# Linear attention and SwiGLU on one core: the weights loaded at other times, and 1/den of two groups spread by PE

## The chip, the core and the metric

The kernel runs on one core of a Trainium2 chip. The metric is the device time of one execution in microseconds. Five engines work beside each other, each with its own queue of instructions that it takes in order: TensorE (PE, the matrix engine), VectorE (DVE), ScalarE (ACT), GpSimd (POOL) and SyncE (SP, which here only issues DMAs). They wait for each other through semaphores.

## The reference

A sequence x of 2048 tokens of 512 numbers in bf16 passes four layers. Layers 0 and 2 are linear attention A, layers 1 and 3 the feed-forward part B, with the same weights both times:

```
phi = lambda t: where(t > 0, t + 1, exp(t)) + 1e-6
A(x): q, k, v = split(x @ wqkv)                 # 32 heads of 16
      kv  = sum_s phi(k)_s v_s^T ;  z = sum_s phi(k)_s          # per head
      o   = (phi(q) @ kv) / (phi(q) @ z + 1e-6)
      return o @ wo
B(x): return (silu(x @ w_gate) * (x @ w_up)) @ w_down            # 512 -> 1792 -> 512
x = x + A(layernorm(x)); x = x + B(layernorm(x)); the same two again
```

The layer norm has neither scale nor offset, with eps 1e-5.

## The kernel before

The sequence is cut into 16 tiles of 128 tokens, four of them to a group of 512. All weights and x stay in SBUF. x is loaded by SyncE, K's part of the weights by ScalarE, Q's part by SyncE behind x, and everything else (V's part `Wv`, `Wo`, `Wg`, `Wu`, `Wd`) by GpSimd in layer 0.

The work is written as operations with reads and writes (`op`, a class `Prog`). The order of PE is written out by hand in the string `PROGRAM`; every other engine's order comes from the kernel's own list scheduler (`schedule`), which takes, among the operations that can start within `HOLD` of the earliest, the one with the smallest due time, shifted by `BIAS` for its kind. `sync` then places the semaphore waits. DMAs of SyncE take turns on eight lanes, and each waits for the one eight before it; GpSimd's take turns on four. `ON_ACT` lists the operations that ScalarE does instead of VectorE.

A token of `PROGRAM` is a layer, a letter and indices. `S` is a matmul of zeros at the start, which nobody reads. The letters:

- `t` (0t0): a tile is transposed by PE (`xt_pe`); tiles that are not in `PE_T` are transposed by a DMA of SyncE from the normalised tile `xnA` or `xnB` into `xnT` (L506).
- `k`: K of a tile, four matmuls, then phi (`phi`: ScalarE exp L539, VectorE L544, then L551, or ScalarE L542 and VectorE L548) into `pk`.
- `g`, `z`: what a tile adds to pk^T x and to the sum of pk. In place of V, the normalised x is summed up, and `v` (`kvt`) multiplies by Wv afterwards, masks the result to single heads on VectorE (L612, `KVT`), and `m` multiplies it by Wo. Both results are copied out of PSUM into `GT` (L599 ScalarE, L602 VectorE).
- `q` (0q03: group 0, quarter 3): Q of a group, and phi into `pq`.
- `d` (0d03): phi(q) times z, that is den. After the fourth quarter of a group VectorE adds 1e-6 (L651) and takes the reciprocal (L654, `rtok`). For each tile ScalarE then writes 1/den 16 times beside itself (L661, `rrep`), a DMA of SyncE transposes this into `RT` (L665), and VectorE multiplies pq by it (L674).
- `w` (0w0): the output of an attention tile, pq times GT; VectorE adds it to x and sums the row up (L696). The next layer's norm follows: ScalarE sums the squares (L473), GpSimd makes mean, variance and rstd (L476, L482, L486), VectorE (L497) or ScalarE (L493) applies them, and the transpose goes to SyncE's queue.
- `u` (1u011: group 0, block 11 of 128 hidden columns), `n`: the FFN, eight matmuls and a tanh each (L716, L718, L721), and the down projection of a tile (L744).

Nearly all matmuls are recorded in the helper `mm`, so they stand under L388; PE's transposes stand under L520. Layer 0's norm takes its sums from VectorE (L462, L464).

The weights that GpSimd loads are held back until one transpose of layer 0 has landed:

```python
last = [o for o in pr.ops if o.kind == "xT"][-1:]
for w_ in weights:
    w_(last)
```

The list is in the order of tiles, so that one is tile 15's, which is not the last that SyncE issues.

## Time and profile before

| what | us |
|---|---|
| median of 6 runs | 435.76 |
| lowest and highest | 433.6, 437.88 |
| the profiled execution: its time | 435.6 |
| its span, from the first to the last instruction | 433.7 |
| PE busy | 420.3 |
| VectorE busy | 294.4 |
| ScalarE busy | 203.0 |
| GpSimd busy | 79.9 |

The span is what the profile covers; 1.9 us of the execution lie around it. An engine's busy time is the union of its instructions. A wait is put down to the semaphore that came last. The chain of waits is followed back from the last instruction, at each step to what released it.

### The profile page before, as it was taken

To read this page: it belongs to the slowest core of one execution; us is meant where nothing else is said; L and a number is where in the kernel's file an instruction comes from. 1 tells how busy PE (TensorE), PEld (TensorE's weight loads), DVE (VectorE), ACT (ScalarE), POOL (GpSimd) and SP (SyncE) were. 2 spreads that over 40 slices of the span, in tenths; PEclk is the share of its full clock that TensorE was granted. 3 is DMA by queue.
4 is the path that set the end of the run, shared out by engine and by line. 5 is a ranking of instruction groups with operands and counts; after the bars stand their busy time and mean duration, and the time that the engine had idled before them with its cause. 6 is when DMAs were issued, how large, how long until landed. Compare 5 with 4: busy or idle time off the path is not lost.

```text
span 433.7 us, 6518 instructions
## 1 busy us (share of the span) xinstructions
PE 420.3 (97%) x2195; PEld 193.5 (45%) x2195; DVE 294.4 (68%) x594; ACT 203.0 (47%) x381; POOL 79.9 (18%) x230
## 2 busy tenths in 40 slices
PE   7997998999999999999999999899999999999997
PEld 3443443444444444444444454344444444444444
DVE  6975789895498457884754548898855617744762
ACT  4875786944454254442525758486322203411320
POOL 5754117303310120002002100642020000000000
DMA  8479644320210010000101105443010010001001
GB/s 279 84 142 369 208 89 82 77 59 14 48 36 2 12 36 2 0 2 12 26 12 24 26 15 104 78 87 73 1 38 24 12 39 12 14 13 36 2 0 50
DMA packets 57249, 24.29 MB, mean 56 GB/s; under 512 B 50752, under 2 KB 56000, under 8 KB 57216
## 3 DMA queue, kind: packets, MB, share of 16 engines
q1 hardware_dynamic: 55232, 16.79, 18.1%
q0 software_dynamic: 1440, 6.55, 4.4%
q10 hardware_dynamic: 544, 0.52, 0.4%
q8 instruction: 18, 0.29, 0.3%
q14 instruction: 15, 0.12, 0.1%
HBM read 9.70 MB, written 2.10 MB: 27 GB/s over the span
## 4 chain that ended last, share of the span: by engine, by line
PE 82%; DMA 5%; DVE 5%; POOL 3%; ACT 2%; issue 2%; SPq 2%; DVEq 0%; ACTq 0%
PE pb L388 82%; DMA xnT<-xnA 2%; POOL rstd L486 1%; SPq L506 1%; DVE X L696 1%; DMA xnT<-xnB 1%; DMA RT<-rrep 1%; DVE pq L674 1%; DMA X<-in_A_x_dram 1%; DVE GT L602 1%; DVE xnB L497 1%; ACT etmp L539 0%; POOL vpe L482 0%; DVE rtok L654 0%; ACT xnA L493 0%
## 5 line engine op out<-in xcount | busy, mean ns | idle before, releaser
L716 ACT ACTIVATE tht<-pb 128x512 f32<-128x512 f32 x112 | 66.6, 594 | 120.1 <-PE pb L388 113.9
L388 PE MATMUL pb<-xnT,Wg 128*128 128x512 bf16 x448 | 115.0, 379 | 1.3 <-DMA xnT<-xnB 1.3
L388 PE MATMUL pb<-xnT,Wu 128*128 128x512 bf16 x448 | 115.0, 379 | 0.0
L388 PE MATMUL pb<-Wd,hT 128*128 128x512 bf16 (+1 forms) x462 | 99.3, 373 | 0.0
L718 DVE SCALAR_TENSOR_TENSOR tht<-tht,pb 128x512 f32<-128x512 f32 x112 | 76.8, 686 | 28.6 <-ACT tht L716 25.9
L721 DVE TENSOR_TENSOR hT<-tht,pb 128x512 bf16<-128x512 f32 x112 | 77.0, 688 | 11.6
L388 PEld LDWEIGHTS pb<-Wd,hT 128*128 128x128 bf16 x462 | 45.2, 98 | 51.5
L388 PEld LDWEIGHTS pb<-xnT,Wg 128*128 128x128 bf16 x448 | 43.7, 98 | 54.3 <-issue 1.8
L388 PEld LDWEIGHTS pb<-xnT,Wu 128*128 128x128 bf16 x448 | 43.8, 98 | 52.9
L476 POOL TENSOR_SCALAR mv<-sums 128x1 f32<-128x1 f32 x48 | 11.4, 242 | 228.7 <-DVE X L696 130.7
L539 ACT ACTIVATE etmp<-pb 128x512 bf16<-128x512 f32 x64 | 38.1, 598 | 30.1 <-PE pb L388 29.7
L486 POOL TENSOR_TENSOR rstd<-vpe,negh 128x1 f32<-128x1 f32 x64 | 36.8, 575 | 5.3
L388 PE MATMUL pb<-Wqkv,xnT 128*128 128x512 bf16 x128 | 31.8, 379 | 3.5 <-DMA xnT<-xnA 3.5
L388 PE MATMUL pb<-GT,pq 128*128 128x512 bf16 x128 | 31.2, 380 | 2.8 <-DVE pq L674 2.4
L744 DVE SCALAR_TENSOR_TENSOR pq<-pb,X 128x512 bf16<-128x512 f32 (+1 forms) x17 | 11.2, 660 | 32.7 <-PE pb L388 32.7
L388 PE MATMUL pb<-xnT,Wqkv 128*128 128x512 bf16 x128 | 32.2, 378 | 0.0
L388 PE MATMUL pb<-pk,xnA 128*128 128x512 bf16 x128 | 31.7, 378 | 0.4 <-DVE pk L551 0.4
L473 ACT ACTIVATE xnB<-X,sums 128x512 bf16<-128x512 bf16 x32 | 22.9, 716 | 14.7 <-DVE X L696 7.5
L544 DVE TENSOR_SCALAR etmp<-etmp 128x512 bf16<-128x512 bf16 x64 | 18.9, 296 | 14.5 <-ACT etmp L539 13.7
L744 DVE SCALAR_TENSOR_TENSOR X<-pb,X 128x512 bf16<-128x512 f32 x16 | 11.1, 692 | 20.5 <-PE pb L388 20.5
L473 ACT ACTIVATE xnA<-X,sums 128x512 bf16<-128x512 bf16 x16 | 11.5, 720 | 23.8 <-DVE X L744 23.7
L661 ACT ACTIVATE rrep<-rtok 128x512 bf16<-128x512 bf16 x32 | 18.7, 622 | 6.7 <-DVE rtok L654 5.1
(63 smaller groups left out, 302.3 us busy)
## 6 DMA issues: line engine op xcount, KB each, us to landing
out_dram<-pq SPq DMA_DIRECT2D x15, 128.0 KB, 1.7
Wg<-in_B_w_gate_dram POOLq DMA_DIRECT2D x4, 448.0 KB, 5.7
Wu<-in_B_w_up_dram POOLq DMA_DIRECT2D x4, 448.0 KB, 5.4
X<-in_A_x_dram SPq DMA_DIRECT2D x6, 256.0 KB, 4.9
Wd<-in_B_w_down_dram POOLq DMA_DIRECT2D x3, 512.0 KB, 5.5
Wqkv<-in_A_wqkv_dram ACTq DMA_DIRECT2D x2, 256.0 KB, 3.5
X<-in_A_x_dram SPq DMA_DIRECT2D x4, 128.0 KB, 3.4
Wqkv<-in_A_wqkv_dram SPq DMA_DIRECT2D x1, 512.0 KB, 6.4
```

The costliest lines, as they stand in the source:

```text
L388: return op("pe", lambda e: e.matmul(o_ap, lhsT=lhsT, rhs=rhs, start=start, stop=stop, skip_group_check=skip), r=r, w=w, occ=occ, lat=occ ...
L473: op("act", lambda a: a.activation(out=b_ap, in_=X[:, t, :], func=ACT.Square, scale=-float(D), bias=sums[:, t:t + 1], accum_out=mv[:, t, 1 ...
L476: op("pool", lambda p: p.tensor_scalar(out=mv[:, t, 0:1], in0=sums[:, t:t + 1], scalar1=-1.0 / D, scalar2=None, op0=ALU.mult), r=[f"sm{t}" ...
L486: op("pool", lambda p: p.tensor_tensor(out=rstd[:, t:t + 1], in0=vpe[:, t:t + 1], in1=negh[:], op=ALU.pow), r=[f"vp{t}", "negh"], w=[f"rs{ ...
L497: op("dve", lambda v: v.tensor_scalar(out=b_ap, in0=X[:, t, :], scalar1=mean, scalar2=rstd[:, t:t + 1], op0=sub, op1=ALU.mult), r=[xk, f"m ...
L539: op("act", lambda a: a.activation(out=etmp[e][:], in_=PB[pb][:], func=ACT.Exp), r=[f"pb{pb}"], w=[f"e{e}"], occ=0.48, lat=0.55, kind="exp")
L544: op("dve", lambda v: v.tensor_scalar(out=etmp[e][:], in0=etmp[e][:], scalar1=1.0, scalar2=1e-6, op0=ALU.min, op1=ALU.add), r=[f"e{e}"], w ...
L661: op("act", lambda a, tl=tl, q=q: a.activation(out=rrep[q][:].rearrange("p (h j) -> p h j", j=DH), in_=rtok[d][:, tl * H:(tl + 1) * H].uns ...
L716: op("act", lambda e: e.activation(out=tht[a][:], in_=PB[pg][:], func=ACT.Tanh, scale=0.5), r=[f"pb{pg}"], w=[f"th{a}"], occ=0.48, lat=0.5 ...
L718: op("dve", lambda v: v.scalar_tensor_tensor(out=tht[a][:], in0=tht[a][:], scalar=1.0, in1=PB[pg][:], op0=ALU.add, op1=ALU.mult), r=[f"pb{ ...
L721: op("dve", lambda v: v.tensor_tensor(out=hT[h][:, j, :], in0=tht[a][:], in1=PB[pu][:], op=ALU.mult), r=[f"pb{pu}", f"th{a}"], w=[f"h{h}_{ ...
L744: op("dve", lambda v, pb=pb, lo=lo, hi=hi: v.scalar_tensor_tensor(out=o_ap[:, lo:hi], in0=PB[pb][:, 0:hi - lo], scalar=0.5, in1=X[:, t, lo ...
```

## The change

- The load of `Wv` goes from GpSimd to SyncE, behind that of Q's weights and ahead of the transposes.
- `Wo`, `Wg` and `Wu` wait for all DMA transposes of layer 0, and stand in the order Wo, four Wg, four Wu in GpSimd's queue.
- `Wd` is loaded by GpSimd after the first four output tiles of layer 0 (`load_down`); its first load waits for the transposes of layer 1's first group.
- Group 2 of layer 0 and group 1 of layer 2 no longer go over `rrep` and the DMA. VectorE transposes `rtok` in blocks of 32 x 32 into `rT`, and PE multiplies `rT` by a constant `esel` (ScalarE writes its four parts once) in four steps `r` of four matmuls each, which spreads 1/den over the 16 columns of a head. VectorE multiplies pq straight from PSUM, in each step the tokens of one block of 32 in every tile. `rep_pe` did this in another form before, and was called by no token.
- Tile 15 of layer 0 is transposed by PE (`0t15`).
- `rrep` has three buffers instead of four.
- PE's order, `ON_ACT`, `BIAS`, `HOLD` and some of the scheduler's estimates are new; with them ScalarE makes the sums of tiles 4 and 8 in layer 0, and VectorE some of the variances. Paths for `raw` tiles and `colsum` are written too; no token uses them.

The diff, cut to its core:

```diff
@@ scheduler's constants, PROGRAM, PE_T, ON_ACT
-HOLD = 0.16
+HOLD = 0.17
...
-S S S S S S S S S 0t0 S S S 0t1 0k0 0t2 0t3 0k1 S 0k2 0z0 0g0 0k3 0g1 0k4 0g2 0g3 0k5 0k9 0z4 0g4 0k10 0g5 0k7
-0z9 0k8 0z2 0q03 0k6 0z7 0g10 0q01 0z8 0k12 0z1 0k15 0k13 0z10 0g9 0z6 0k11 0z3 0q11 0g7 0k14 0z15 0z11 0z5
-0q02 0z13 0q12 0z12 0q21 0z14 0g11 0q00 0q13 0d02 0d03 0q10 0g8 0d00 0g6 0d01 0q20 0d13 0g13 0q22 0d10 0d12
-0d11 0d20 0g12 0q23 0g14 0g15 0q30 0d22 0d21 0d23 0v 0q31 0m0 0m2 0m1 0m3 0q32 0w0 0w2 0q33 0w3 0d32 0w1 0w9
-0w6 0d30 0w10 0w5 0w4 0w7 0d33 0w11 0w8 0d31 1u011 1u009 1u002 1u000 1u012 1u004 1u007 1u005 1u003 1u006 1u013
...
+S S S S S S S S S 0t0 S S S S 0t3 0t1 0k0 0t2 0k1 0k2 0g0 0k3 0z0 0g1 0k4 0g2 0g3 0k5 0z4 0k10 0z2 0k9 0g4 0g5
+0k6 0z10 0k7 0z9 0z3 0q03 0k8 0g10 0t15 0g7 0k15 0k13 0z5 0z8 0k12 0g9 0k11 0q11 0g6 0z15 0k14 0q10 0z13 0q02
+0z7 0z1 0q01 0g11 0q00 0z14 0q12 0q21 0z12 0z6 0z11 0q13 0d02 0d03 0d01 0d00 0g8 0d11 0q20 0g13 0d12 0q22 0d13
+0d10 0q23 0d20 0g15 0g12 0g14 0d23 0d22 0d21 0q30 0v 0q31 0m0 0m1 0m3 0m2 0r21 0r23 0w3 0r22 0w2 0w1 0r20 0w0
+0q33 0w5 0w11 0w7 0w6 0w9 0q32 0d33 0w8 0w4 0w10 1u011 1u007 1u005 1u008 0d31 1u002 1u006 0d32 1u012 1u003
+1u013 0d30 1u010 1u004 1u000 1u110 1u001 1u009 0w14 1n3 0w12 1n0 1u106 1n1 1u102 1n2 1u107 1u204 0w13 1u101
...
-2q31 2g13 2d12 2g8 2q30 2g11 2g15 2g10 2d23 2g9 2q32 2v 2q33 2m1 2m0 2m3 2d31 2m2 2d32 2w0 2w1 2w2 2w3 2w10
-2d30 2w7 2w6 2d33 2w4 2w8 2w11 2w9 2w5 3u008 3u007 3u002 3u000 3u010 2w14 3u004 3u011 3u009 3u005 3u013 3u006
-3u012 3u001 3u103 3u003 3u110 3u108 3u104 2w13 3n3 2w12 3u100 3n2 3n0 3u106 3u105 3u107 3u111 3n1 3u102 3u109
...
+2d22 2q30 2d10 2d12 2g13 2g10 2d11 2d23 2q31 2g15 2g4 2g9 2g11 2g8 2q32 2r10 2v 2q33 2m1 2m0 2m2 2m3 2w0 2d31
+2r11 2d30 2w1 2r13 2w2 2w3 2r12 2w6 2w5 2w11 2w4 2w8 2w7 2d32 2w9 2w10 2d33 3u008 3u000 3u009 3u013 3u010
+3u004 3u003 3u005 3u007 3u103 3u110 3u108 3u012 3u002 3u001 3u006 3u104 2w13 3u011 3n3 2w12 3u100 3n2 3n0
...
 PE_T = set("""
-0t0 0t1 0t2 0t3
+0t0 0t1 0t2 0t3 0d2 0t15 2d1
 """.split())
...
-        rrep = [sb("rrep", [P, 512], BF16) for _ in range(4)]
+        rT = [sb("rT", [P, TG * H], BF16) for _ in range(2)]
+        esel = sb("esel", [P, H, DH], BF16) if any(x[1] == "d" for x in PE_T) else None
+        rrep = [sb("rrep", [P, 512], BF16) for _ in range(3)]
...
+            for i in range(0, P if esel is not None else 0, H):
+                op("act", lambda a, i=i: a.activation(
+                    out=esel[i:i + H], in_=ident[i:i + H, i:i + H].unsqueeze(2).to_broadcast([H, H, DH]),
+                    func=ACT.Copy), r=["ident"], w=[f"esel{i // H}"], occ=0.52, after=after)
...
         dma("sp", Wqkv[:, :, 0:D], wq3[:, :, 0:D], 512, w=["Wq"], prio=-80)
-        weights.append(lambda a: dma("pool", Wqkv[:, :, 2 * D:], wq3[:, :, 2 * D:], 512, w=["Wv"], after=a,
-                                     occ=1.0))
+        dma("sp", Wqkv[:, :, 2 * D:], wq3[:, :, 2 * D:], 512, w=["Wv"], prio=-79)
...
-        for c in range(0, NF, 4):
-            c1 = min(NF, c + 4)
-            weights.append(lambda a, c=c, c1=c1: dma(
-                "pool", Wd[:, c:c1, :], B_w_down[c * P:c1 * P, :].rearrange("(c p) f -> p c f", p=P),
-                128 * (c1 - c), w=[f"Wd{j}" for j in range(c, c1)], after=a, occ=0.75))
+
+        def load_down(after):
+            for c in range(0, NF, 4):
+                c1 = min(NF, c + 4)
+                dma("pool", Wd[:, c:c1, :], B_w_down[c * P:c1 * P, :].rearrange("(c p) f -> p c f", p=P),
+                    128 * (c1 - c), w=[f"Wd{j}" for j in range(c, c1)], after=after, occ=0.75)
...
             if f"{L}d{g}" in PE_T:
+                op("dve", lambda v: v.transpose(out=rT[d][:], in_=rtok[d][:]), r=[f"rtok{d}"], w=[f"rT{d}"],
+                   occ=0.2, lat=0.3, kind="den")
                 return
...
-        def rep_pe(L, g, tl):
+               occ=0.335, lat=0.42, kind="pqn")
+
+        def rep_pe(L, g, a):
 
             pb = bank()
             d = db[L, g][1]
             r_den.done(d)
+            ps = slice(a * H, (a + 1) * H)
             for c in range(NC):
-                lo = tl * H + c * HC
-                mm(pb, rtok[d][:, lo:lo + HC].unsqueeze(2).to_broadcast([P, HC, DH]), ident[:], True, True,
-                   r=[f"rtok{d}", "ident"], w=[f"pb{pb}"], occ=MM128, cols=(c * P, (c + 1) * P), skip=True)
-            scale(L, g, tl, PB[pb][:].rearrange("p (c k) -> p c k", c=NC), f"pb{pb}", 0.607)
+                mm(pb, esel[ps, c * HC:(c + 1) * HC, :].rearrange("p h j -> p (h j)"), rT[d][ps, :], True, True,
+                   r=[f"rT{d}", f"esel{a}"], w=[f"pb{pb}"], occ=MM128, cols=(c * P, (c + 1) * P), skip=True)
+            b = pq_of[L, g]
+            ks = [f"pq{b}_{j}_{tl}" for j in range(NC) for tl in range(TG)]
+            ap = pq[b][:].rearrange("p c (t a i) -> p c t a i", t=TG, a=P // H)[:, :, :, a]
+            by = PB[pb][:].rearrange("p (c t i) -> p c t i", c=NC, t=TG)
+            op("dve", lambda v: v.tensor_tensor(out=ap, in0=ap, in1=by, op=ALU.mult),
+               r=ks + [f"pb{pb}"], w=ks, occ=0.607, lat=0.69, kind="pqn")
...
-        last = [o for o in pr.ops if o.kind == "xT"][-1:]
+        last = [o for o in pr.ops if o.kind == "xT"]
...
+                if tok in head:
+                    head.discard(tok)
+                    if not head:
+                        load_down([xT_of[1, t] for t in range(TG) if (1, t) in xT_of])
```

## The prediction

> **What bounds the kernel now.** I read the page from the top: busy shares, slices, then the waits of PE, then the chain around the longest wait, then single rows for prices.
>
> ```profile
> PE 420.3 (97%) x2195; PEld 193.5 (45%) x2195; DVE 294.4 (68%) x594; ACT 203.0 (47%) x381; POOL 79.9 (18%) x230
> PE   7997998999999999999999999899999999999997
> DMA  8479644320210010000101105443010010001001
> ```
>
> PE is busy 97%. In the 20 us windows between 100 and 260 us it is busy all the time, with 93 to 95 large matmuls in each: 0.214 to 0.216 us per 128x512 matmul, at a granted clock of 1.00. There nothing can be gained or lost but matmuls. The slices that are not nines are the head, two stages of layer 0 (20 to 40 us and 55 to 73 us), the same second stage of layer 2 (slice 24, 260 to 283 us), and the tail. The change is worth what it does there.
>
> ```profile
> PE pb L388 <- DMA xnT<-xnA: 3.5, 2, 2.6
> PE pb L388 <- DVE pq L674: 2.4, 6, 0.6
> PE pb L388 <- DMA xnT<-xnB: 1.3, 2, 1.0
> ```
>
> The waits of PE (us in total, times, longest) name three causes: a DMA transpose of layer 0, the scaling by 1/den, and the first transposes of layers 1 and 3. The chain shows where the longest comes from:
>
> ```profile
> 27.52 0.97 POOL Wqkv L415
> ...
> 28.50 0.76 POOL Wo L415
> ...
> 29.60 0.57 POOL rstd L486
> ...
> 30.27 0.42 DVE xnA L497
> ...
> 30.76 6.83 DMA xnT<-xnA
> 37.59 0.14 issue
> 37.73 2.50 PE pb L388 x25
> ```
>
> GpSimd issues the loads of Wv and Wo before it makes the last tile's rstd; that tile's transpose is issued at 30.76, runs beside the weights, and lands after 6.83 us where the median is 2.4. Step 0k14 waits for it.
>
> **A. From the start to 0v (55.07 us before).** I measure in starts of PE's steps. Between 0k4 (14.10) and 0v lie 40.97 us. Four gaps in it, start to start less the matmuls between (0.864 us per four): 0.19 before 0g2, 0.52 before 0g5, 1.12 before 0k6, 2.74 before 0k14; together 4.57. Work is 36.40.
>
> *Removed.* In the new order GpSimd's first load stands behind the last rstd and waits for all eleven transposes. Tile 15 goes by PE, so eleven are left. They need 1.31 us each in SP's queue (issue to issue where they follow closely); the fourth was issued at 16.46, so by their inputs the last comes at about 25 to 27 and lands by 30. 0k14 now stands 20 large steps behind 0k4, after 32 us: its 2.74 us go. 0k6 waited for the transpose issued at 20.81, which landed after 4.89 us; a 16 KB packet of the instruction queue at 22.0 lies in that stretch. Tile 6 is now the fifth transpose, due at about 18.5, and 0k6 stands at about 22: that wait goes too. What is late next is 0k8 (seventh transpose, 22 undisturbed, 24.4 with the same delay), wanted at about 25: just covered.
>
> *Added.* Four PE transposes for 0t15: 0.24 (0t1 to 0k0: 7.73 to 7.97). The head: 0t3 now stands before 0t1 and waits for the rstd of tile 3, which GpSimd makes after tile 1's; 0k0 moves from 7.97 to about 8.8. Four warm-up matmuls stand behind 0t0 instead of three, but the one before 0k2 is gone. ScalarE takes the sums of tiles 4 and 8 (two Copy and two Square passes at about 0.71) before its copy of 0t3; I get 0k4 at 14.8 by following ScalarE's queue, 0.7 late.
>
> Wv goes on SP's queue behind Wq, ahead of the first transpose. Here a rule speaks against the change. Row: Wq landed at 12.10, 1.45 after the last of x; the first transpose was issued at 11.25, with Wq still moving, and landed at 13.81, after 2.56 instead of 2.44. So a load ahead in the queue cost it 0.12. Wv will move until about 13.55. The Trainium skill (DMA: Bandwidth & Descriptors, "Two DMAs through the same engine are not ordered") says that within one queue of an engine descriptors start in order, but pipelined. By that the transpose starts behind Wv and lands at 13.55 + 2.44 = 15.99, and 0k4 at 16.1; by the row it lands between 13.9 and 15.25. I take the row's middle, 14.6, so 0k4 stays at 14.8. The rule's value would add 1.3 us.
>
> ScalarE's work up to 0v grows: two more normalisations (0.72), four passes for sums, four constants `esel` (0.52 by the slot of L661), less three Identity passes (0.575) and one spread: +4.1 us. It was about 36 busy of 47. I allow 0.3 of new waits; ends 0 and 3. VectorE gets 0.5 less. The weight loads, 4.15 MB at the 260 GB/s of before (4.67 MB from 27.5 to 45.4), run from 29 to about 45.5: Wo and Wg are first wanted after 52 and 67, so they cost nothing; the first spread's transpose comes only then.
> A = −4.57 + 0.24 + 0.7 + 0.3 = −3.3; I use −3.2.
>
> **B. 0v to the first FFN step, layer 0.** Before 55.07 to 73.40 = 18.33 us, with PE's work 15.1.
>
> ```profile
> 55.00:74.00 19.00, 16.68 (x108) 7.89 (x105) 17.29 (x49) 13.95 (x30) 7.46 (x23) 1.00 0.48 89
> 265.00:283.00 18.00, 15.79 (x94) 6.64 (x92) 16.06 (x43) 11.25 (x25) 7.42 (x22) 1.00 0.42 81
> ```
>
> The windows (length; then busy us of PE, PEld, VectorE, ScalarE, GpSimd; clock, DMA share, GB/s) show VectorE busy 91% and 89%: it is the near-bound of both stages, and SP's transposes stand in one queue of 1.31 us each.
>
> Group 2 loses four spreads on ScalarE, four transposes on SP (4 x 1.31 = 5.2 us of that queue) and four scalings from SBUF; it gains a VectorE transpose, 16 matmuls 128x128 on PE and four scalings from PSUM.
>
> ```profile
> L661 ACT ACTIVATE rrep<-rtok 128x512 bf16<-128x512 bf16 x32 | 18.7, 622 | 6.7 <-DVE rtok L654 5.1 <-DMA RT<-rrep 1.5
> L674 DVE TENSOR_TENSOR pq<-pq,RT 128x512 bf16<-128x512 bf16 x32 | 13.0, 417 | 2.1 <-DMA RT<-rrep 2.0
> L721 DVE TENSOR_TENSOR hT<-tht,pb 128x512 bf16<-128x512 f32 x112 | 77.0, 688 | 11.6
> ```
>
> Prices. The matmuls: 0v's 16 of that size took 55.07 to 55.96, so 0.9 us per group. The scaling: L674's 417 ns against L721's 688 for a product with PSUM, 4 x 0.27 = 1.1 us more of VectorE per group. The Trainium skill (VectorE: DVE Perf Modes, "The perf-mode tier table") gives bf16 products from SBUF twice the rate of any with PSUM; that would be 4 x 0.417 = 1.7 per group, against the change. The row decides; the sum by the rule is 1.2 us worse over both layers if VectorE is bound. The VectorE transpose has no row: not below 0.1, not above the reciprocal's 0.95 on the same 128x128; I take 0.29, as the 128x128 pass before it (L651).
>
> Following VectorE's and PE's orders with these slots from 0v on (us after 0v): mask of KVT done 1.7, the four 0m 1.75 to 2.6, evacuations of GT until 3.55, so 0w3 waits 0.55 (before, 0q32 covered this); 0w5 at 8.5, 0w11 9.3 (its four scalings done at 9.0), 0w7, 0w6 and 0w9 follow, 0q32 12.8, 0w8, 0w4 and 0w10 until 16.3. The last transpose the FFN needs, 0w0's, is issued at 13.3 and lands by 15.7. VectorE's work in the stretch is 17.6, of which the last results may run into the FFN. So 16.3, I use 16.5: B = −1.8. Three of the four den steps of group 3 move into the FFN: **C** = +0.3.
>
> Wd is loaded here: GpSimd stops until the four transposes of layer 1's first group have landed, at the FFN's start (about 68), then issues four loads, which took 9.1 us before (41.36 to 50.49). Behind them in GpSimd stand rstd of tiles 7, 5, 11 and on. Their transposes are wanted at 1u110, 13 FFN steps of 1.727 later, about 91; even if none moves during these 9 us the sixth lands at about 88.5. Wd itself is wanted at 1n3, about 97. Cost nothing, covered by 2.5 us at worst.
>
> **D. The same stage of layer 2.** Before 265.28 (2v) to 282.42 = 17.14. In the new order 2r10 stands before 2v (0.25); 2w0 waits 1.0 for the evacuations, 2w6 0.9 for the last scaling from PSUM (8.9 us after 2v), then nothing: FFN at 16.0. −1.14 + 0.25 = −0.9; I use −0.7, since one wait before (2w10) lay beside an instruction fetch at 270.0, which may strike elsewhere.
>
> **Sum.** −3.2 − 1.8 + 0.3 − 0.7 = −5.4. The profiled execution took 435.6 (span 433.7 and 1.9 around it): 430.2. The median of the runs shown is 435.76, 0.2 above; I leave it at 430.2, −1.3%.
>
> **Rivals.** 1. *VectorE is the bound in B and D.* For: 91% and 89% busy before, and 1.1 + 0.3 us more per group. Against: SP's queue is 5.2 us shorter, and residual sums may run over. B and D give nothing and 0.7 of the added matmuls shows: 435.6 − 3.2 + 0.3 + 0.7 = 433.4.
> 2. *ScalarE, or Wv in front of the transposes, sets the pace of A.* For: +4.1 us on a queue that was 89% busy from 10 to 20 us, and the rule above. Against: its first waits are for PE. A shrinks to −0.6: 432.8.
> 3. *Slower: the scaling from PSUM in pieces.* One instruction takes every fourth run of 32 columns; the trace has only runs of 128 (L674) and whole rows (L721). The eight of them stand in VectorE's queue before the residual sums that free PE's banks. Each us more goes straight onto PE: 430.2 + 8 x (d − 0.69), slower than before once d exceeds 1.36 us; at 1.7 it is 438.3, and the delayed first transposes of layers 1 and 3 add about 2: 440. For it speaks only that no row shows such a pattern.
> That the change does not act as said (a fetch of instructions meets other transposes, which cost 0.5 to 1.1 of PE each time) moves every case by 1 to 2.
>
> **Chances.** Forecast 0.58, own range 427.5 to 431.4; rival 1 0.19; rival 2 0.15; rival 3 and the like 0.08. The runs before lie between 433.6 and 437.9, so about 1% is what this measurement tells from no change: below 431.4 is faster, above 440.1 slower. Faster 0.58, within 1% 0.34, slower 0.08. Range 427 to 435.5: the forecast's ends, both middle rivals, and the upper bounds of ScalarE's waits and of Wv; rival 3 is left out.
>
> **What will show it.** A right: no wait of PE on xnT<-xnA over 0.5, 0k4 at 14.5 to 15.5, 0v near 51.9, loads of weights from 27 to 30. B and D right: 16 to 17 us from 0v and 2v to the FFN, the new scaling near 690 ns. C right: PE without gaps at 90 to 100 us. Wrong: the scaling above 1 us, 0k4 past 16.5, or a new wait on GpSimd behind Wd.

## The result and the profile after

The changed kernel takes 432.68 us (median of 34 runs, 431.6 to 435.27) where the kernel before took 434.65 on the same chips (69 runs, 433.26 to 439.31): a ratio of 0.9949, 95% interval 0.9936 to 0.9962. The forecast was 430.2, 5.4 us below its base of 435.6; between the medians lie 2.0. A run's time goes with its mean granted clock: it is below 0.999 in 31 of the 95 runs of the kernel before beside the experiments and in 7 of the 34 here, and the medians of the kernel before on the four chips are 434.2 to 435.1 us at 1.00 and 435.5 to 437.2 at 0.996. The profiled execution took 432.6, its span 430.9.

The page of the changed kernel, busy shares and two rows of the slices:

```profile
PE 421.1 (98%) x2231; PEld 194.5 (45%) x2231; DVE 290.7 (67%) x593; ACT 214.9 (50%) x402; POOL 80.0 (19%) x231
...
PE   6999999999999999999999999999999999999997
...
DMA  8649234632210020000111104242020210001001
```

The slices that were not nines at 20 to 40 us, in the first of the two stages behind the KVT products and in the second are nines now. ScalarE has 11.9 us more to do, VectorE 3.7 less. The waits of PE (us in total, times, longest):

```profile
PE pb L539 <- DVE xnA L513: 1.8, 1, 1.8
PE pb L395 <- DVE hT L401: 1.2, 1, 1.2
PE pb L539 <- DVE mv L480: 1.1, 1, 1.1
PE pb L395 <- DVE pq L742: 0.9, 1, 0.9
PE pb L395 <- DMA xnT<-xnB: 0.6, 1, 0.6
PE pb L395 <- DVE tht L775: 0.6, 2, 0.4
PE pb L395 <- ACT etmp L558: 0.4, 1, 0.4
PE pb L395 <- ACT GT L649: 0.4, 1, 0.4
```

The 3.5 us on the layer 0 transposes (`xnT<-xnA`) are gone, as forecast, and of the 2.4 on the scaling by 1/den 0.9 are left. What stands at the head is longer (1.8 and 1.1, against 0.9 and 0.3 before), and two rows the forecast did not have: 0.6 on the transposes of layer 1 and, new, 0.6 on `tht`, an FFN product.

The two stages behind the KVT products, in windows of 17 us each (length; then busy us of PE, PEld, VectorE, ScalarE, GpSimd; clock, DMA share, GB/s):

```profile
53.00:70.00 17.00, 16.99 (x103) 7.71 (x101) 16.52 (x45) 12.99 (x28) 6.60 (x21) 1.00 0.33 65
263.00:280.00 17.00, 15.74 (x107) 7.55 (x107) 16.06 (x44) 10.72 (x23) 7.28 (x23) 1.00 0.30 59
```

In the first, PE has no idle time left, with VectorE busy 97%. The groups of the spread (busy us, mean ns; idle before):

```profile
L713 ACT ACTIVATE rrep<-rtok 128x512 bf16<-128x512 bf16 x24 | 14.3, 625 | 1.3 <-DVE rtok L704 0.9 <-DMA RT<-rrep 0.4
...
L726 DVE TENSOR_TENSOR pq<-pq,RT 128x512 bf16<-128x512 bf16 x24 | 9.8, 418 | 0.0
L742 DVE TENSOR_TENSOR pq<-pq,pb 128x512 bf16<-128x512 bf16 x8 | 5.5, 683 | 0.4 <-PE pb L395 0.3
...
L707 DVE STREAM_TRANSPOSE rT<-rtok 128x128 bf16<-128x128 bf16 x2 | 0.6, 311 | 0.1
```

The scaling from PSUM in pieces of 32 columns takes 683 ns (0.69 was used), 1.63 times the 418 of the one from SBUF and not twice as much; VectorE's transpose takes 311 ns (0.29 was used).

**Where the time went**, by starts of PE's steps. The kernels of the experiments are measured by the same stages: 0k0 is the first k projection, A the time from the start to 0v, B from 0v to the first gate product of layer 1, C from there to the first down product, E from there to 2v, D from 2v to the first gate product of layer 3; the last 151.2 us behind that are the same everywhere to 0.3. In nine of the traces below the record of the first matmul of that down product is missing: the first one recorded starts 0.43 us after the matmul before it, where 0.216 is the step, and there are 13 of 14. There C and E are counted from the missing one, 0.22 us earlier; the expectations counted from the first recorded.

| us | 0k0 | A | B | C | E | D | span |
|---|---|---|---|---|---|---|---|
| before | 7.97 | 55.07 | 18.33 | 26.76 | 165.12 | 17.14 | 433.7 |
| after | 9.26 | 52.72 | 16.36 | 28.75 | 165.54 | 16.25 | 430.9 |
| after less before | 1.29 | −2.35 | −1.97 | +1.99 | +0.42 | −0.89 | −2.8 |
| forecast | 0.8 | −3.2 | −1.8 | +0.3 with E | | −0.7 with 2r10 (which lies in E) | −5.4 |

So 2.6 us are missing, nearly all of it in two stages: 1.7 in C, where Wd now moves, and 0.85 in A. B and D look as forecast. The experiments say which of these four readings holds; B's and D's reasons fared worse than their numbers.

### The profile page after: what moved, and what is told of

The parts are those of the page before. It is cut to its first block, busy times and chain, and to the rows that moved or that the text cites. A ratio compares the mean times of both kernels' runs of the same rounds, so it can differ in the third digit from the quotient of the medians.

```text
span 430.9 us, 6541 instructions
## 1 busy us (share of the span) xinstructions
PE 421.1 (98%) x2231; PEld 194.5 (45%) x2231; DVE 290.7 (67%) x593; ACT 214.9 (50%) x402; POOL 80.0 (19%) x231
## 4 chain that ended last, share of the span: by engine, by line
PE 88%; ACT 3%; DMA 3%; POOL 2%; issue 1%; DVE 1%; SPq 0%; ACTq 0%; DVEq 0%
PE pb L395 88%; DMA xnT<-xnB 2%; POOL rstd L502 1%; ACT xnA L509 1%; DMA X<-in_A_x_dram 1%; ACT xnB L509 1%; POOL nmr L506 1%; POOL vpe L498 0%; ACT etmp L558 0%; DVE tht L775 0%; ACT pk L561 0%; DVE stats L478 0%; ACT tht L773 0%; SPq L522 0%; ACT xnB L489 0%
## 5 line engine op out<-in xcount | busy, mean ns | idle before, releaser
L492 POOL TENSOR_SCALAR mv<-sums 128x1 f32<-128x1 f32 x50 | 11.9, 241 | 200.9 <-DVE X L753 113.4
L558 ACT ACTIVATE etmp<-pb 128x512 bf16<-128x512 f32 x64 | 37.2, 595 | 14.7 <-PE pb L395 12.2
L502 POOL TENSOR_TENSOR rstd<-vpe,negh 128x1 f32<-128x1 f32 x64 | 36.6, 572 | 32.4 <-DVE vpe L498 28.4
L489 ACT ACTIVATE xnB<-X,sums 128x512 bf16<-128x512 bf16 x32 | 22.9, 715 | 14.0 <-DVE X L753 6.2
L509 ACT ACTIVATE xnA<-X,nmr,rstd 128x512 bf16<-128x512 bf16 x23 | 18.6, 811 | 10.7 <-POOL nmr L506 10.6
L801 DVE SCALAR_TENSOR_TENSOR X<-pb,X 128x512 bf16<-128x512 f32 x16 | 11.1, 692 | 18.8 <-PE pb L395 18.7
L753 DVE SCALAR_TENSOR_TENSOR X<-pb,X 128x512 bf16<-128x512 f32 x32 | 21.5, 685 | 0.8 <-PE pb L395 0.7
```

The source lines that it names most:

```text
L489: op("act", lambda a: a.activation(out=b_ap, in_=X[:, t, :], func=ACT.Square, scale=-float(D), bias=sums[:, t:t + 1], accum_out=mv[:, t, 1 ...
L492: op("pool", lambda p: p.tensor_scalar(out=mv[:, t, 0:1], in0=sums[:, t:t + 1], scalar1=-1.0 / D, scalar2=None, op0=ALU.mult), r=[f"sm{t}" ...
L502: op("pool", lambda p: p.tensor_tensor(out=rstd[:, t:t + 1], in0=vpe[:, t:t + 1], in1=negh[:], op=ALU.pow), r=[f"vp{t}", "negh"], w=[f"rs{ ...
L509: op("act", lambda a: a.activation(out=b_ap, in_=X[:, t, :], func=ACT.Identity, bias=nmr[:, t:t + 1], scale=rstd[:, t:t + 1]), r=[xk, f"nm ...
L558: op("act", lambda a: a.activation(out=etmp[e][:], in_=PB[pb][:], func=ACT.Exp), r=[f"pb{pb}"], w=[f"e{e}"], occ=0.48, lat=0.55, kind="exp")
L753: op("dve", lambda v: v.scalar_tensor_tensor(out=X[:, t, :], in0=PB[pb][:], scalar=1.0, in1=X[:, t, :], op0=ALU.mult, op1=ALU.add, accum_o ...
```

## The experiments

Each is compared with the kernel before, run beside it on the same chip. The kernel before had medians of 434.5 to 436.8 on these chips, so that ratios are compared and not medians alone; the stages come from one profiled execution of each, which may lie off its kernel's median. Every edit also lets the scheduler plan the other engines' queues anew; where that matters it is said.

### 1. Where Wd is loaded

What C shows in the changed kernel. Wd is issued at 70 to 74 us and its packets move from 71.6 to 78.5. Three transposes of layer 1 are issued in that time, at 75.28, 76.56 and 77.88, and land after 5.2, 4.4 and 5.0 us, where the four later ones take 2.4. The chain of waits from 66 to 99 us, cut to its longer pieces:

```profile
73.37 0.57 POOL rstd L502
...
74.39 0.82 ACT xnB L509
...
75.28 1.19 SPq L522
...
76.56 4.38 DMA xnT<-xnB
...
81.15 0.20 ACT xnB L489
...
88.36 0.82 ACT xnB L509
...
89.24 2.41 DMA xnT<-xnB
...
91.79 7.28 PE pb L395 x33
```

In this chain the slow transpose releases ScalarE and not PE: `xnB` is a ring of three buffers, and the Square pass of the next tile (L489) waits until a transpose has emptied one. ScalarE's own list of waits in that window:

```profile
ACT xnB L489 <- DMA xnT<-xnB: 4.4, 2, 3.4
```

Behind that Square pass, in ScalarE's order, stand the tanh passes that empty PE's banks, and the normalisation of the tiles whose transposes are wanted last. PE shows it as gaps of 0.36 and 0.21 inside gate and up products and 0.64 before 1u110; counted from start to start, less the 0.216 of a matmul, they are 0.52, 0.37 and 0.80, together 1.70. The theory: Wd lengthens the transposes, and the ring hands that to ScalarE. Rivals: the transposes are slow for another reason; or Wd's issue holds up GpSimd.

**Wd behind gate and up, in layer 0.**

```
         for w_ in weights:
             w_(last)
+        load_down(last)
...
-                        load_down([xT_of[1, t] for t in range(TG) if (1, t) in xT_of])
+                        pass
```

> The changed kernel, with Wd loaded behind Wu in layer 0 as before, all else in the same order. Theory 1: the gaps inside 1u0 vanish (-1.7 us), but Wd moves from about 45 to 52 us and meets the transposes of 1/den of groups 0 and 1 (47 to 61 us), so 0w3 and what follows may wait: between -1.7 and +1 against the changed kernel, 431.0 to 433.7. Theory 2 (order of PE): gaps stay, 432.7 or more.

Measured: 431.97 us (431.31 to 434.26), ratio 0.9945 (0.9921 to 0.9968); C 27.06, B 16.94. C falls by 1.69 us, and both waits of PE leave the list. ScalarE's, VectorE's and SP's queues hold the same instructions in the same order as in the changed kernel, so that Wd's place is all that differs: it is the cause of these 1.69. The three transposes still take 3.3, 4.1 and 3.1 us with no weight under way: they follow each other at 1.3 us, and two packets of the instruction queues (8 and 16 KB, at 76.9 and 78.2) lie between them. By difference Wd accounts for about 1.9, 0.3 and 1.9 us of their delay, not for all of it. B is 0.58 longer, and 0.9 in the two other kernels below with Wd early. Wd is now under way until 50.5 us, beside the first transposes of 1/den (3.6 us the first); that this makes B longer is not shown, since a later one (3.5) lies beside a packet of the instruction queue.

**Wd behind the second group of layer 1 too.**

```
-        head = set(f"0w{t}" for t in range(TG))
+        head = set(f"0w{t}" for t in range(2 * TG))
...
-                        load_down([xT_of[1, t] for t in range(TG) if (1, t) in xT_of])
+                        load_down([xT_of[1, t] for t in range(2 * TG) if (1, t) in xT_of])
```

> The changed kernel, with Wd held until the eight transposes of layer 1's groups 0 and 1 have landed instead of four. Theory 1 (Wd's transfer slows the transposes of group 1 and, through the three xnB buffers, ScalarE's queue): the gaps of PE inside 1u0 (0.36, 0.21, 0.64 us) vanish, from 1u011 to 1n3 27.1 instead of 28.75 us, transposes of tiles 5, 7 and 11 land after 2.4 instead of 4.4 to 5.2 us; time 1.7 us under the changed kernel, about 431.0. Wd is then needed at 1n3 and must land by about 96; if it doesn't, the wait is at 1n3 and says so. Theory 2 (the new order of PE and the den steps inside the FFN make these gaps): they stay, time 432.7.

Measured: 435.43 us (432.76 to 438.67), ratio 1.002 (0.999 to 1.0049). C is 27.35, but E is 170.62, 5.1 more. Wd is issued at 90 us, and two transposes of 1/den, issued at 90.60 and 92.31, take 6.5 and 9.8 us beside it. PE's list now begins with Wd itself:

```profile
PE pb L395 <- DMA Wd<-in_B_w_down_dram: 2.4, 3, 1.1
```

The wait went on to the next transposes, and Wd came too late as well. Of the 5.1, up to 1.7 are no wait: from 101.5 us PE's granted clock is 0.50 for 3.4 us (last section).

**The change's place for Wd in the kernel before.** `load_down` as in the change, all else as before.

> The kernel before, with only Wd's load moved into the FFN behind the transposes of layer 1's group 0. Theory 1: the same slow transposes (4 to 5 us) and gaps of PE in 1u0 of 1 to 2 us; time 434.6 + 1 to 2 = 435.6 to 436.6. Theory 2 (the gaps belong to the new order): no gaps, 434.6.

Measured: 436.95 us (435.06 to 440.94), ratio 1.006 (1.0029 to 1.009); C 30.79 against 26.76. Moving Wd into the FFN, which the forecast priced at nothing, costs 4.0 us in C here, of which A, 0.45 shorter, and D, 1.04 shorter, give some back in this profile. D's part is chance: there every queue has the same order as before.

**Own row buffers in layers 1 and 3.** The rows go into the 16 buffers of layers 0 and 2, which are free then; Wd stays where the change put it.

```
-            if L % 2 == 0:
-                b_ap, bk = xnA[:, t, :], f"xa{t}"
-            else:
-                b = r_xb.take(1)
-                b_ap, bk = xnB[b][:], f"xb{b}"
+            b_ap, bk = xnA[:, t, :], f"xa{t}"
```

> The changed kernel, with the normalised rows of layers 1 and 3 written into the 16 row buffers that layers 0 and 2 use, in place of a ring of three; Wd's loads stay where the change put them. Theory (Wd's loads lengthen the transposes of the normalised rows at 75 to 83 us, and through the ring ScalarE, which waits for a free buffer with the activations of gate and up queued behind it): ScalarE's wait of 3.4 us for a transpose goes, the gaps of 0.36 and 0.21 us inside the first gate and up products go, the next transposes are issued 2 to 4 us earlier and the wait of 0.64 us for one goes too; the stretch from the first gate product to the first down product falls from 28.75 us to 27.4 to 27.8, and the median is 431.3 to 431.8. Rival (the transposes are late for TensorE whatever ScalarE does): the three transposes still take 4.4 to 5.2 us, the stretch stays at 28.4 or above and the median at 432.4 to 433.

Measured: 430.89 us (430.48 to 431.72), ratio 0.9895 (0.9865 to 0.9926); C 27.06. Without the ring nothing holds the transposes back, and they become slower still: eight in this stretch, with a median of 6.5 us from issue to landing.

```profile
L516 SPq DMA_TRANSPOSE xnT<-xnA x8: 1188/1203/2768, 72.3 to 86.8; - x8
...
DMA to landing us min/median/max: 2.4/6.5/11.5
```

No PE wait on them is left, since all eight are issued by 87 us instead of 89 and more; and ScalarE waits for no transpose of rows, but for PE and the steps of the normalisation:

```profile
ACT tht L767 <- PE pb L395: 3.4, 5, 1.2
ACT xnA L485 <- DVE X L747: 3.1, 2, 2.8
ACT xnA L505 <- POOL nmr L502: 2.6, 4, 1.2
```

So transposes of up to 11.5 us cost PE nothing where no in-order queue waits for them. The rival (they are late for PE whatever ScalarE does) expected 28.4 or more; the other rival, GpSimd held up by Wd's issue, fails too, since GpSimd issues Wd at 70.6 to 74.3 us here as well. One thing is not separated: without the ring the scheduler also puts ScalarE's and GpSimd's passes from 66 to 90 us in another order. That Wd costs the 1.69 is shown with the order kept (Wd in layer 0); that it does so by the ring rests on the chain above and on this run together.

**The same once more.**

> The changed kernel with own row buffers once more. If its gain is the 1.47 us that its profile shows in the FFN: a ratio to before of 0.991 to 0.993. If the first measurement stands: 0.987 to 0.991. If that one was an accident and the buffers are worth nothing: 0.994 to 0.996.

Measured: 430.79 us (430.59 to 431.24), ratio 0.9867 (0.983 to 0.9904), C 27.06. It has the lowest median of all and beats both the changed kernel and the one before. It lies 1.9 us under the changed kernel's median, and 1.6 among the runs with a full granted clock alone (430.79 against 432.37), which the 1.69 of C cover. The lower ratio is that of a chip on which the kernel before ran at 436.78.

**Both repairs of C.** Own row buffers, and Wd in layer 0.

> The changed kernel with both repairs of the stretch from the first gate product to the first down product: own row buffers in layers 1 and 3, and Wd loaded behind gate and up in layer 0. Theory (both take away the same loss of about 1.4 us): the stretch is 27.2 to 27.4 us and the median 430.6 to 431.3, that of the kernel with its own row buffers alone. Rival (the slow transposes cost time elsewhere too, as the early ones no longer pass Wd): 429.6 to 430.5.

Measured: 432.05 us (431.46 to 433.19), ratio 0.9949 (0.9933 to 0.9966). C is 27.06, as with either alone; but B is 17.39, 0.93 over that of the own buffers with Wd late. Once the ring is away, Wd early saves nothing in C and only has its cost in B.

**The ring in the kernel before.**

> The kernel before with own row buffers in layers 1 and 3 and nothing else. Theory (without Wd beside them the ring held nothing up): the stretch from the first gate product to the first down product stays at 26.6 to 26.8 us, the median within 0.5 us of before, 434.0 to 435.0. Rival (the ring costs time whatever the loads do): 432.5 to 433.8, and the gain of the own buffers has little to do with the change.

Measured: 435.44 us (433.11 to 439.12), ratio 0.9984 (0.9948 to 1.002); C 26.76, not a hundredth other than before. The ring cost nothing in C as long as no weights moved beside the transposes: the change made it dear.

### 2. What the loads do in A, and what PE's new order does

**The loads held back, alone.** In the kernel before, all of GpSimd's loads wait for all transposes of layer 0 instead of the last one made; Wv and Wd stay among them.

```
-        last = [o for o in pr.ops if o.kind == "xT"][-1:]
+        last = [o for o in pr.ops if o.kind == "xT"]
```

> The kernel before, with only the hold of GpSimd's loads changed: they wait for all transposes of layer 0. Theory A (the hold alone takes the 2.74 us before 0k14): that wait goes, the other waits of the K stage stay; but Wv to Wd, 6.5 MB, then run from about 29 to 54 us, beside the first transposes of 1/den, which costs up to 2 us in the stage of 0w. Time 431.8 to 433.8. If the gain of the K stage came from the order of PE instead, 0k14 waits still and the time is 434.6.

Measured: 442.86 us (440.57 to 444.79), ratio 1.0182 (1.0148 to 1.0217). The wait before 0k14 goes, but the weights now move from 32 to 62 us, and the first transposes of 1/den, issued from 45.60 to 51.05, take 12 to 15.5 us beside them:

```profile
PE pb L388 <- DVE pq L551: 8.2, 1, 8.2
```

What PE waits for is the map of q, a pass of VectorE; it stands in VectorE's order behind a scaling that waits for these transposes. Then PE's granted clock is 0.50 from 53.4 us on, for 10.2 us. The forecast of 431.8 to 433.8 missed by 9 us. The hold paid where Wv and Wd, a third of these bytes, went elsewhere; which of the two matters was not tried.

**All three moves of loads, alone.** In the kernel before: the hold above, Wv on SP's queue, Wd in the FFN; PE's order, the split of the engines and the spread of 1/den as before.

> The kernel before with the change's loads alone: Wv on SP's queue behind Wq, the loads on GpSimd behind all layer 0 transposes, Wd once the first four transposes of layer 1 are through. TensorE's order and the spread of 1/den stay those of before. Theory (the loads make the gain up to the KVT products, and Wd's new place costs as much again in the FFN as it did when it alone was moved, 2.3 us): the waits of 2.74 and 1.12 us for layer 0's transposes go, the first product with KVT comes at 54 to 55 us in place of 57.44, the stretch from the first gate product to the first down product is 29.5 to 31 us in place of 26.76, and the median is 433.8 to 435.2. Rival (without the new order of TensorE the weights, which now start at 31 us, run into the transposes of 1/den as they did when the loads were only held back): a wait for 1/den of 4 us or more, and a median of 438 to 442.

Measured: 432.39 us (431.45 to 435.89), ratio 0.9962 (0.9943 to 0.9981): its interval overlaps that of the whole change, so that, with the ring in place, no gain in time of the new order and the spread beyond the loads is shown. The profiled execution took 434.68, 2.3 above this median, and its stages may be longer than the usual ones. A is 51.06 us, 4.01 less than before and 1.66 less than in the changed kernel. B (18.10) hardly moves, and C is 30.16: the loss behind Wd is 3.4 us here. The waits of PE from 66 to 100 us:

```profile
PE pb L388 <- DVE tht L717: 3.1, 2, 2.4
PE pb L388 <- DMA xnT<-xnB: 0.9, 1, 0.9
PE pb L388 <- DVE pq L673: 0.2, 1, 0.2
```

**The loads, with own row buffers.**

> The kernel before with the change's loads alone, and own row buffers in layers 1 and 3. Theory (the ring carries Wd's interference to ScalarE here as well): the stretch from the first gate product to the first down product falls from 30.16 us to 26.8 to 27.8, and the median to 429 to 430.5. Rival (TensorE waits for the transposes themselves, since its order is the old one): 29 us or more and 431.8 to 432.8.

Measured: 433.62 us (431.9 to 436.34), ratio 0.9927 (0.9892 to 0.9963). The forecast of 429 to 430.5 failed, and against the loads alone no gain in time is shown. The changed kernel with own row buffers, on the same chip, ran at 430.79 (430.59 to 431.24): there the new order and the spread do gain. C is 28.70, between what the two theories expected. ScalarE no longer waits for rows, but now VectorE does for 1/den, and PE behind it:

```profile
DVE pq L667 <- DMA RT<-rrep: 4.8, 1, 4.8
...
PE pb L388 <- DVE tht L711: 1.8, 1, 1.8
```

In the old order a transpose of 1/den is issued at 77.84, beside Wd, and takes 7.4 us; the scaling that waits for it stands in VectorE's queue ahead of an FFN product. In the changed order the first of these goes at 91.41, when Wd has landed. PE's own wait for rows is 0.4.

**The head's order.** Tiles 0, 1, 2, 3 are transposed by PE in that order, in the changed kernel, with 0k0 behind tile 1 and one warm-up matmul less:

```
-S S S S S S S S S 0t0 S S S S 0t3 0t1 0k0 0t2 0k1 0k2 0g0
+S S S S S S S S S 0t0 S S S 0t1 0k0 0t2 0t3 0k1 0k2 0g0
```

> The changed kernel, with the TensorE transposes of the first four row tiles in the order 0, 1, 2, 3 of the kernel before, one k projection between them, in place of 0, 3, 1, 2. Theory (the first k projection starts 1.29 us later than before because it now stands behind the transpose of tile 3, whose rows are normalised later): the first k projection starts at 8.0 to 8.6 us, half of it or more is given back in waits for tile 3 before the fifth k projection, and the median is 431.7 to 432.4. Rival (the head is paced by the chain of normalisation on VectorE and ScalarE, not by TensorE's order): the fifth k projection stays at 15.2 to 15.4 us and the median at 432.5 to 432.9.

Measured: 433.0 us (432.45 to 433.17), ratio 0.9943 (0.9923 to 0.9963). 0k0 starts at 7.95, as before the change, and 0k4 at 14.64 in place of 15.29; yet 0v comes at 52.66 in place of 52.72. All that was won at 0k0 is given back by 0v. C is 29.36 here and 29.44 in the next kernel, 0.6 and 0.7 over the changed kernel, so what Wd costs there is not the same in every kernel with the ring.

**The sums of tiles 4 and 8 on VectorE.** `0s4 0s8` are taken out of `ON_ACT`.

> The changed kernel with the sums of row tiles 4 and 8 on VectorE, as those of the other tiles, in place of two Copy and two Square passes on ScalarE. Theory (at the head ScalarE's passes stand before its evacuations of the transposed tiles 3 and 2 and set its pace): the fifth k projection starts at 14.5 to 14.9 us in place of 15.29, and the median is 432.0 to 432.5. Rival (VectorE is as full there, so the two statistics passes of 0.69 us only change the queue): 15.1 to 15.8 us and a median of 432.6 to 433.3.

Measured: 433.29 us (432.42 to 434.13), ratio 0.9973 (0.9959 to 0.9986); 0v at 52.82. No gain either.

**The head in order and Wd early.** The edit of the head's order above and Wd behind gate and up in layer 0.

> The changed kernel with Wd loaded behind gate and up in layer 0, and the TensorE transposes of the first four row tiles in the order 0, 1, 2, 3. If both mend what they are meant to (1.3 us of the stretch from the first gate product to the first down product, 0.3 to 1.0 us of the head), the sum stands beside the changed kernel's 432.7: 430.4 to 431.4. If the order at the head is worth nothing, it equals the kernel with Wd early alone: 431.5 to 432.1.

Measured: 432.26 us (431.92 to 433.23), ratio 0.9935 (0.9909 to 0.9961); 0v at 52.78, B 17.30, C 27.07: Wd early alone, and nothing from the head.

### 3. The spread by PE, and the order around it

**The new order without the spread.** `0d2` and `2d1` are taken out of `PE_T`, and the eight `r` steps out of the order. The two groups (group 2 of layer 0, group 1 of layer 2) go through ScalarE and SP again. The rows for 1/den stay three, and ScalarE's list of waits for 50 to 73 us has none on them.

> The changed kernel, with 1/den of the last group of each attention layer spread by DMA transposes again, as the kernel before does it; TensorE's order is otherwise the changed one's. Theory (the spread by TensorE makes the gain of the two stretches from the KVT products to the FFN, 1.97 and 0.89 us): these stretches come back to 18.0 to 18.6 and 16.9 to 17.5 us, less some 0.6 us of spreading products that TensorE no longer runs, and the median is 434.5 to 435.3. Rival (the new order of TensorE makes the gain there, the spread is idle weight): the stretches stay near 16.4, and the median is 431.9 to 432.8.

Measured: 439.25 us (438.45 to 441.1), ratio 1.0089 (1.0055 to 1.0123); B 21.89 and D 19.04, 5.5 and 2.8 us over the changed kernel. Far more than the theory asked for:

```profile
PE pb L395 <- DVE pq L726: 7.3, 2, 4.3
```

PE stands before the output steps of the group that lost the spread, 4.27 us in layer 0 and 3.05 in layer 2; in layer 0 the group's last transposes land at 67.25 and 69.85, and the scaling by the last one runs at 71.4. And behind each of the two waits PE's granted clock is about half for 3.4 us (the third figure from the end of a row is the clock):

```profile
65.30:68.70 3.40, 3.40 (x9) 1.21 (x8) 1.31 (x5) 0.81 (x2) 1.26 (x3) 0.50 0.42 83
280.30:283.70 3.40, 3.18 (x8) 1.16 (x8) 2.06 (x6) 1.24 (x3) 1.12 (x4) 0.51 0.40 77
```

Eight products of 128x512 in the first follow each other at 0.43 us in place of 0.216. So some 1.7 us of each stage are the clock and not the wait itself.

**The spread in the old order.** From 0v and 2v to the first FFN products PE goes in the order of the kernel before, with the `r` steps put between, one by one:

```
0v 0q31 0m0 0m2 0m1 0m3 0r20 0q32 0r21 0w0 0r22 0w2 0r23 0q33 0w3 0d32 0w1 0w9 0w6 0d30 ...
```

> The changed kernel with the steps from 0v to the first FFN products, and from 2v to those of layer 3, in the order of the kernel before; the four spreading steps of the changed group stand one by one between them, ahead of the first output step that needs them. With the kernel without the spread it makes the other half of a two by two. Theory (spread and order work only together: the new order asks for the changed group's rows early, which only the spread has ready, and the spread brings little where the rows are asked for late): from the first product with KVT to the first gate product 15.5 to 16.5 us in layer 0 (14.43 in the changed kernel, 15.96 before) and some 15 in layer 2, median 433.6 to 434.8. Rival (the spread alone relieves SP's queue and is the gain, whatever the order): 14.4 to 15.1 us, median 432.4 to 433.2.

Measured: 434.69 us (433.29 to 439.49), ratio 1.002 (0.9994 to 1.0046). The four corners of this two by two (us), all with the changed loads; the first is the kernel with the loads alone, which also has the old order ahead of 0v, four spread rows and the old split of the engines:

| | B, old order | B, new order | D, old order | D, new order |
|---|---|---|---|---|
| transposes on SP | 18.10 | 21.89 | 16.81 | 19.04 |
| spread by PE | 18.42 | 16.36 | 16.42 | 16.25 |

In layer 0 the spread alone loses 0.3 and the order alone 3.8, about 1.7 of it by the clock; together they win 1.7. The new order asks for the rows of the changed group early, and only the spread has them ready then.

**The old order up to 0v, the new one and the spread behind it, own row buffers.** It also leaves out the PE transpose of tile 15 and has the old split of engines up to 0v.

> The changed loads, TensorE's order and the split between VectorE and ScalarE up to 0v as in the kernel before (three transposes of the head and no fifth for tile 15, all sums on VectorE), the changed kernel's order and its spread of 1/den from 0v on, and own row buffers in layers 1 and 3. Theory (the parts add): the first product with KVT comes at 53.3 to 54 us as with the loads alone, the first gate product 14.4 to 14.9 us later as in the changed kernel, the first down product 27.3 us after that, and the median is 1.2 to 1.8 us below that of the changed kernel with own buffers, 428.8 to 430.3. Rival (the new order behind 0v rests on work that the new order ahead of 0v has done earlier): 16 us or more to the first gate product, median 431 to 433.

Measured: 431.79 us (431.62 to 432.29), ratio 0.9889 (0.9852 to 0.9926). A is 52.00, B 17.33, C 27.06: the parts do not add up; 51.1 and 16.4 would have been their sum. Up to 0v it differs from the kernel with the loads alone in the four `esel` constants on ScalarE (0.63 us each in the changed kernel), the ring of three in place of four spread rows and the planner's costs. Of the 0.9 us in A, 0.38 are there at 0k0 already; what makes the rest is open.

## Why the prediction was half right

**A, forecast −3.2, came −2.35.** The mechanism was right and the larger part was even shown alone: no PE wait on `xnT<-xnA`, the eleven transposes landed by 28.63, the weights issued from 29.29 us, and −4.01 us with the loads alone where 4.57 of waits were to go. Of the weighing of row and rule for Wv, the row held: the first transpose, issued at 11.61, landed at 14.39 (14.6 was taken from the row; 15.99 was drawn from the rule, whose "pipelined" does not exclude the overlap seen), while Wv landed at 13.83. The term that was mis-sized is the head's, "I get 0k4 at 14.8 by following ScalarE's queue, 0.7 late": 0k4 came at 15.29, 1.19 late. The waits after it were 0.79 where 0.3 was allowed. Neither PE's order nor the split of the sums alone cost it: with tile 1 first, 0v came no earlier, and neither did it with the sums on VectorE. The stretch from 0k0 to 0v is 43.46 us in the changed kernel and 43.04 with the loads alone; of these 0.42 the fifth PE transpose was priced at 0.24. The other 1.24 of the 1.66 that A lost against the loads alone is the later start of 0k0. Which engine paces the head so that both repairs are given back stays open. A part of the 0.85 may be chance: two kernels with the same queues as the changed one up to 0v, own row buffers once more and Wd behind the second group, reach 0v at 52.71 and 52.01.

**B, forecast −1.8, came −1.97.** The number was right, in part by luck, and so were the prices (683 ns, 0.9 us of matmuls a group, 16.36 us from 0v to the FFN). The reason was half of one: the working let VectorE and SP's queue be relieved and followed the new order with that. The two by two shows no clear gain from the relief in the old order (18.10 and 18.42 us in layer 0). Rival 1 (VectorE is the bound) is not what happened in the changed kernel; VectorE is 97% busy there, but PE has no idle time.

**C, forecast +0.3, came +1.99, and this is the step that failed:** "Wd itself is wanted at 1n3, about 97. Cost nothing, covered by 2.5 us at worst." The bound asked when the transposes land and when PE wants them. It held almost in its own terms: the last wanted one landed at 91.65 for a step wanted at 91. What it left out is that a transpose also has to free a buffer, that the next pass in ScalarE's order waits for this buffer, and that ScalarE's tanh for PE's banks stand behind that pass. Of the 1.99, 0.3 are the den steps, as forecast; the other 1.69, priced at nothing, went when Wd was moved away and as much with the ring. The named sign for a failure, "a new wait on GpSimd behind Wd", was the wrong queue.

**D, forecast −0.7, came −0.64 with the 0.25 of 2r10 counted, and the reason did not hold.** Two kernels that keep the old spread and the old order there take 16.02 (own row buffers in the kernel before) and 16.10 (Wd late in it), less than the changed kernel's 16.25. The second has every queue in the same order there as the kernel before, so that its 1.04 are chance. What probably made the 17.14 of before is how two transposes fell, at 268.14 and 269.45, beside a packet of 16 KB of the instruction queue at 270.0: 4.07 and 3.13 us. From issue to landing in the window from 262 to 280 us, first the kernel before, then the same with own row buffers:

```profile
DMA to landing us min/median/max: 2.4/2.5/4.1
```

```profile
DMA to landing us min/median/max: 2.4/2.5/3.7
```

In the kernel before VectorE's scaling waited for the first of these, 1.8 us; in the other the packet fell on a later pair. No run moved the packet alone. The forecast saw it and took 0.2 off; against stages of 16.0 to 16.1 the spread gains nothing here. The old stage takes 16.0 to 17.3 us in the kernels that kept it, and the profile of before lay near the upper end; that may be why the profiles differ by 2.8 us and the medians by 2.0.

**The sum.** With the ring away the changed kernel runs at 430.8, within 0.6 us of the forecast: the sum had one large cost too few. That it comes so close is partly luck, since the base of 435.6 lay 0.95 above the median of the kernel before. Of the rivals, number 2 has the nearest time (432.8), but not by its cause: A was short by 0.85 and not by 2.6. Number 3 did not occur, since the scaling takes 0.683 us.

## What to carry to other kernels

When a load is moved next to other transfers, follow each transfer that it slows to everything that its end releases: not only the step that wants its data, but the buffer it frees, the instruction that waits for that buffer, and all that stands behind this instruction on its engine. It need not be one engine: with the ring gone from the old order, VectorE waited in ScalarE's place. A moved weight load has to go somewhere; here every place (with the first loads, in layer 0, in the FFN, later) lay beside some transposes, and the cheapest was the one where nothing in order waited for them. And before a gain is booked against a stage of one profile, see whether a chance delay in that execution makes it: other kernels with the same stage show what it takes undisturbed.

## What the runs showed of the hardware

Transposes from SBUF to SBUF on SP's queue and weight loads on GpSimd's queue slow each other. Alone, a transpose of 128x512 takes 2.4 us from issue to landing. Beside the four loads of Wd it took 4.4 to 5.2 us when the ring held the stream back, up to 11.5 when it did not, and 12 to 15.5 beside the last loads of gate, up and Wd. The loads suffer too: Wd, issued from 70 to 74 us in both, had landed at 79.1 with three transposes beside it and at 85.2 with six. The queues in the window from 69 to 89 us of the kernel with own buffers (packets, MB, share of 16 engines):

```profile
q0 software_dynamic: 512, 1.84, 43.0%
q1 hardware_dynamic: 4381, 1.05, 40.9%
```

So the 1.05 MB of the transposes take nearly as much of the engines' time as the 1.84 MB of Wd, and together they fill 84% of the window. The packets of the transposes are of some 240 bytes, those of Wd of 3.6 KB. The Trainium skill (DMA: Bandwidth & Descriptors, "Queues, rings and completion order") says that a DMA engine takes turns between queues by packets; a stream of small packets would then wait for a large one at each turn. These numbers agree with that, but no run changed the size of a packet, and none shows that the page's packets are those of the profile.

Single packets of the instruction queues, 8 or 16 KB, coincide with transposes of 3.1 to 4.1 us where nothing else moves (76.9 and 78.2 us with Wd early, 270.0 before). Not every one does: in the changed kernel one of 16 KB at 57.1 us leaves the transposes around it at 2.4 and 2.5. Where they fall differs from kernel to kernel.

After some waits PE's granted clock is half for 3.4 us or a multiple of it: in the kernel without the spread after 4.27 and 3.05 us, with all loads held back for 10.2 us in a wait of 8.25, with own row buffers at 8.3 us in a wait of 2.10 at the head, and in the kernel before with own row buffers after one of 2.10 before 0k14. Others as long were not followed by it: 2.57 us before 0k14 in the kernel before, 2.39 with the loads alone, 3.17 with Wd late in the kernel before. What decides is not shown. One such stretch makes a mean clock of 0.996 (3.4 x 0.5 of 430 us), so that a wait taken away can be worth more than its length. No term of the forecast had this.
